# Top-32 attention into a gelu MLP: paired search in two early slots, reordered work in slot 4 and in the first pair of slots

## The chip, the core and the metric

The kernel runs on one core of one Trainium2 chip. The metric is the device time of one execution in microseconds (us), and the time of a kernel is the median over its runs. A separate, profiled execution gives the trace: it records the instructions of each engine with start and duration. The engines are TensorE (PE, whose weight loads are listed as PEld), VectorE (DVE), ScalarE (ACT), GpSimd (POOL) and SyncE (SP, which issues most of the DMAs here).

## The reference

Attention over 8 batches and 8 heads, with 576 positions of 64 numbers, in which each row keeps only its 32 largest scores; the heads are then joined to rows of 512 numbers, and these go through a two-layer MLP with the quick gelu:

```python
scores = scale * q @ k.T                              # (8, 8, 576, 576), scale = 1/sqrt(64)
kth = np.partition(scores, -32)[..., -32]             # 32nd largest of each row
attn = softmax(where(scores >= kth, scores, -1e9))
x = (attn @ v).transpose(0, 2, 1, 3).reshape(8 * 576, 512)
h = x @ w_in                                          # (4608, 2048)
out = (h * (1 / (1 + exp(-1.702 * h)))) @ w_out       # (4608, 512)
```

All is float32.

## The kernel before

**Slots.** The attention is cut into 144 slots. A slot is one tile of 128 rows for one pair of heads; the last 64 rows of four heads make an "ends" slot, so a batch has 18. For slot n the stages are these, each on one engine:

- PE multiplies q by k into two PSUM tiles `s_ps` (`scores`, L295), and ACT copies them scaled to `sc` (`copy_scores`, L307).
- DVE finds the 32 largest of each row. In slots 0 to 10 `topk` does this on all 576 columns: 8 MAX8 (L317) that each find the next eight values, and 6 MATCH_REPLACE8 (L320) that remove them. From slot 11 on `topk_of_pairs` does it on pairs of columns: DVE takes the `greater` of columns j and j + 288 (L336), POOL the `lesser` by two integer operations on the bit patterns (L339 in `pair_up`, L349 in `pair_rest`); then 8 MAX8 and 6 removals on the greater, 4 MAX8 and 2 removals on the lesser (288 columns each, L366 and L369), and two small reductions that merge both lists and give the bound (L373, L378).
- POOL derives the row's bounds `cut` and `low` (`bounds`, L410 and L411, in the early slots; `lows`, L399, for paired slots, whose `cut` comes from DVE).
- ACT masks what lies below the bound (`mask`, L423) and takes the exponentials with their sums (`exps`, L431).
- The sum is inverted on DVE (`invert`, L439 and L441). In the early slots `divide` has POOL make a diagonal matrix of the inverses (L448), with which PE turns the probabilities (`turn_main`, `turn_ends`, L468 and L471) and ACT copies the result `pt` out (L476). In paired slots POOL multiplies the probabilities themselves (`normalize`, L454), ACT splits them into 16-bit halves (`split`, L490), and two DMAs by way of DRAM turn them (`turn_by_dma`, L498).
- PE multiplies by v (`values`, L526; `values_at`, L557), and ACT copies the result into `xT` (L539, L574).

**MLP.** When 128 rows of x are complete for all heads they make a `Block`. `hidden` computes four blocks of 128 hidden features (two for two blocks at a time) into a PSUM tile `ph` (32 matmuls, L618); `tanh` runs on ACT (L640, with a copy of h at L643); `gate` multiplies, either on DVE (L655) or, with `aside`, on POOL (L652, L653); `project` adds the product with w_out to the block's tile `po` (8 matmuls at L673). After 16 feature blocks `po` is complete, ACT copies it out as `ob` (L681) and a DMA stores it.

**PSUM.** `ps_s` has two tiles for scores, `ps_t` has two for turned tiles, values, and some `ph`, `ps_h` has one for `ph`, and `ps_p` one for `po`. A block whose projection begins while `ps_p` holds another takes `ps_h`; while `ps_h` is so taken, `hidden` uses `ps_t`.

**Weights.** Both weight matrices come as 32 pieces that are loaded during slots 0 to 11 and rounded there: `size` (L151), `low` (L154) and `sign` (L153) on ACT, `shift` (L152) on DVE, and two `finish` operations on POOL (L144 and L147). The helper `finish_one` issues the next of the queued finish operations.

**Order.** Each engine works through its instructions in the order in which the program emits them; the kernel writes that order by hand. `slot(n)` emits one early slot: exponentials of n-1, score copies of n+1, then the search of n with pieces of POOL's work between its steps, then PE's turns and values. `two_slots(n)` does the same for slots n and n+1 from n = 11 on; its first call, at n = 11, has `opens` set. SETTLED is 10, PAIRED 11, TURNS 4. `later` holds loads and preparations by slot. `stay_warm` issues matmuls whose result nobody reads. The engines' instructions wait for each other on semaphores where data or a buffer is needed.

Of the kernel before, what the change touches and what calls it, by code (L numbers as in the profile page):

```python
# [11 lines left out]
F32 = mybir.dt.float32  # L12
# [6 lines left out]
P = 128  # L19
# [11 lines left out]
def kernel(  # L31
# [52 lines left out]
    TURNS = 4  # L84
    SETTLED = 10
    PAIRED = SETTLED + 1
    assert D == 64 and 2 * TAIL == P and C == NP * P and C == PIECE and B % 2 == 0
    assert TOPK == 32 and NP == 4 and NF == 4 and NG == 4 and CC == 4

# [241 lines left out]
    def pair_up(n):  # L331

        sc = st[n]["sc"]
        a, b = sc[:, :, 0:HALF], sc[:, :, HALF:S]
        greater[n] = lefts.tile([P, 2, HALF], F32, name="greater", tag="left")
        nc.vector.tensor_tensor(out=greater[n][:], in0=a, in1=b, op=ALU.max)  # L336
        lesser[n] = raws.tile([P, 2, HALF], F32, name="lesser", tag="raw")
        whole = lesser[n][:].bitcast(I32)
        nc.gpsimd.tensor_tensor(out=whole, in0=a.bitcast(I32), in1=greater[n][:].bitcast(I32), op=ALU.subtract)  # L339
        unpaired.append(n)  # L340
# [10 lines left out]
    def topk_of_pairs(n):  # L351

        top = st[n]["top"] = small.tile([P, 2, 2 * TOPK], F32, name="top2", tag="top")
        cut = st[n]["cut"] = small.tile([P, 2], F32, name="cut")
        first, few = greater.pop(n), lesser.pop(n)
        left = lefts.tile([P, 2, HALF], F32, name="left2", tag="left")

        def found(r, i, written=False):
            if r < TOPK // 8:
                at = (8 * r + TOPK) % (TOPK + TOPK // 2)  # L360
                return top[:, i, at : at + 8]
            end = 2 * TOPK - 8 * (r - TOPK // 8) - TOPK
            return top[:, i, end - 1 : end - 9 : -1] if written else top[:, i, end - 8 : end]

        def largest(src, r, i):
            nc.vector.max(found(r, i, True), src[:, i, :])  # L366

        def remove(to, src, r, i):
            nc.vector.match_replace(to[:, i, :], found(r, i), src[:, i, :], LOWEST)  # L369

        def merge():
            both = top[:, :, 0:TOPK].rearrange("p i (s k) -> p i k s", s=2)
            nc.vector.tensor_reduce(  # L373
                out=top[:, :, TOPK + TOPK // 2 :], in_=both, axis=mybir.AxisListType.X, op=ALU.max
            )

        def bound():
            nc.vector.tensor_reduce(  # L378
                out=cut[:], in_=top[:, :, TOPK + TOPK // 2 - 1 :], axis=mybir.AxisListType.X, op=ALU.min, negate=True
            )  # L380

        ops = []
        for r in range(TOPK // 8):
            ops += [lambda r=r, i=i: largest(left if r else first, r, i) for i in range(2)]
            if r < TOPK // 8 - 1:
                ops += [lambda r=r, i=i: remove(left, left if r else first, r, i) for i in range(2)]
        ops += [lambda: pair_up(n + 1) if n + 1 < N else None]
        for r in range(TOPK // 8, TOPK * 3 // 16):
            ops += [lambda r=r, i=i: largest(few, r, i) for i in range(2)]
            if r == TOPK // 8:  # L390
                ops += [lambda r=r, i=i: remove(few, few, r, i) for i in range(2)]
        return ops + [merge, bound]
# [9 lines left out]

    def bounds(n):

        if n >= PAIRED:
            return lows(n)
        top = st[n]["top"]
        cut = st[n]["cut"] = small.tile([P, 2], F32, name="cut")
        low = st[n]["low"] = small.tile([P, 2], F32, name="low")
        nc.gpsimd.tensor_scalar(cut[:], top[:, :, TOPK - 1], -1.0, None, op0=ALU.mult)  # L410
        nc.gpsimd.tensor_tensor(out=low[:], in0=top[:, :, TOPK - 1], in1=top[:, :, 0], op=ALU.subtract)  # L411
# [245 lines left out]
            )  # L657
        to_project.append((th, g, blocks))

    def project(put_off_leaving=False):  # L660

        gT, fs, blocks = to_project.pop(0)
        for x in blocks:
            if not x.done:
                home = "ps_h" if "ps_p" in in_use else "ps_p"
                in_use.append(home)
                x.home = home
                pool_of, tag = (ps_h, "ph") if home == "ps_h" else (ps_p, "po")
                x.po = pool_of.tile([P, C], F32, name="po", tag=tag)
        i = 0  # L670
        for f in fs:
            for x in blocks:
                nc.tensor.matmul(  # L673
                    x.po[:], lhsT=gT[:, i * P : (i + 1) * P], rhs=wout[:, f, :], start=(x.done == 0), stop=(x.done == FC - 1)
                )
                x.done += 1
                i += 1

        def leave(x):
            ob = thp.tile([P, C], F32, name="ob", tag="th")  # L680
            nc.scalar.mul(out=ob[:], in_=x.po[:], mul=0.5 / RAISE**2)  # L681
            for on, to in x.rows:
                nc.sync.dma_start(to, ob[on, :])

        for x in blocks:
            if x.done == FC:
                in_use.remove(x.home)
                leaving.append(lambda x=x: leave(x))
        if not put_off_leaving:
            leave_all()  # L690
# [125 lines left out]
    def slot(n):  # L816

        todo = later.pop(n, [])
        for fn, args in todo:
            if fn is not prepare and fn is not prepare_by_dma:  # L820
                fn(*args)
        preparing = [(fn, args) for fn, args in todo if fn is prepare or fn is prepare_by_dma]
        some = [round_piece(x) for x in by_slot.get(n, [])] if n else early
        if n == 0:
            for piece in some:
                piece["low"]()
                piece["sign"]()
        else:
            bounds(n - 1)
            exponentials(n - 1, bring_all if n % 4 == 1 else lambda: None)  # L830
            copy_scores(n + 1)
            bring_all()
            while signs:
                signs.pop(0)()
            if 1 < n <= TURNS:
                turn_main(n - 2)
                turn_ends(n - 2)
            for piece in some:
                piece["size"]()
            tanh(False)  # L840
        for i, op in enumerate(topk(n)):
            op()
            if i == 2:
                for _ in range(min(3 if n >= TURNS else 6, len(unfinished))):
                    finish_one()
            if i == 5:
                if n > 0:
                    divide(n - 1)
                while unfinished:
                    finish_one()  # L850
            if i == 10:
                gate(False)
        if n == SETTLED:
            pair_up(n + 1)
            pair_rest()
        for piece in some:
            piece["shift"]()
            unfinished.extend(piece["finish"])
        if n < NP:
            for fn, args in preparing:  # L860
                fn(*args)
        if n >= TURNS:
            turn_main(n - 1)
            turn_ends(n - 1)
        if n > 0:
            for piece in some:
                piece["low"]()
        scores(n + 2)
        if n == SETTLED:
            copy_scores(n + 2)  # L870
        if n == 0:
            return
        for i, piece in enumerate(some):
            if n == TURNS and i > 0:
                signs.append(piece["sign"])
            else:
                piece["sign"]()
        idle = not ready and n < TURNS
        if 1 < n <= TURNS:
            values(n - 2, put_off if n == TURNS else None)  # L880
        if n >= TURNS:
            values(n - 1, put_off)
        if n >= NP:
            for fn, args in preparing:
                fn(*args)
        if n > PROJECTS and may_project(2):
            project(n == SETTLED)
        if idle:
            stay_warm(8)
        hidden()  # L890
# [12 lines left out]
    def two_slots(n):  # L903
# [27 lines left out]
        def measure(m):  # L931
            if live(m):
                lows(m)
            pair_rest()
            gate(aside)

        def project_one():
            if may_project(0):
                project(True)

        if opens:
            bounds(n - 1)
            gate(aside)
        if ahead:
            scores(n + 2)
# [26 lines left out]
        for piece in some:  # L972
            piece["shift"]()
            piece["low"]()
            piece["sign"]()
            unfinished.extend(piece["finish"])
        if live(n - 1):
            split(n - 1)
        begin(todo[0])
# [32 lines left out]
            turn_by_dma(n)  # L1012
        tanh(aside)
        measure(n + 1)
        project_one()
        leave_all()

# [38 lines left out]
```

## Time and profile before

| | |
|---|---|
| runs before | 1456.97, 1457.24, 1457.88 us; median 1457.24 |
| profiled execution | 1456.39 us, of which the span of the trace is 1454.6 |
| granted clock of TensorE, mean | 0.986 of full speed |
| first search of slots 1, 2, 3, 4, 5, 6 begins at | 19.72, 30.30, 41.21, 52.13, 63.13, 76.43 us |
| first pair of slots (11 and 12) | about 133 to 165 us |
| a pair of slots later on | about 18.8 us |

Times in a trace are counted from the start of its span. A line of the timeline gives start, duration, engine, line, operation, out<-in and tile, with xcount where several are joined, and in brackets the engine's idle time before it and who ended that. The chain of waits is followed back from the last instruction of its stretch: at each step to what released it, or to the instruction before it on its engine. Engines that share a stretch overlap, so a chain tells which of them set the end, and busy shares alone do not.

### The profile page before, as it was taken

To read this page: it belongs to the slowest core of one execution; us is meant where nothing else is said; L and a number is where in the kernel's file an instruction comes from. 1 tells how busy PE (TensorE), PEld (TensorE's weight loads), DVE (VectorE), ACT (ScalarE), POOL (GpSimd) and SP (SyncE) were. 2 spreads that over 40 slices of the span, in tenths; PEclk is the share of its full clock that TensorE was granted. 3 is DMA by queue.
4 is the path that set the end of the run, shared out by engine and by line. 5 is a ranking of instruction groups with operands and counts; after the bars stand their busy time and mean duration, and the time that the engine had idled before them with its cause. 6 is when DMAs were issued, how large, how long until landed. Compare 5 with 4: busy or idle time off the path is not lost.

```text
span 1454.6 us, 29079 instructions
## 1 busy us (share of the span) xinstructions
PE 1416.5 (97%) x9524; PEld 996.4 (68%) x9524; DVE 1362.5 (94%) x4681; ACT 1158.9 (80%) x1862; POOL 977.6 (67%) x1177
## 2 busy tenths in 40 slices
PE   7789799999999999999999999999999999999998
PEld 5667466777666667777666667777666667777665
DVE  7999999999999999999999999999999999999910
ACT  6998787888888887888888888888878888777730
POOL 3788766766677777666777777766777767667610
PEclk8899899999999999999999999999999999999999
DMA  7442467777777867777677767767677776645430
GB/s 224 136 161 75 127 154 191 189 189 180 176 198 184 188 170 191 186 198 177 170 194 182 183 170 195 202 174 189 166 203 189 180 182 179 161 133 130 138 89 15
DMA packets 521272, 244.40 MB, mean 168 GB/s; under 512 B 457376, under 2 KB 495264, under 8 KB 521120
## 3 DMA queue, kind: packets, MB, share of 16 engines
q1 hardware_dynamic: 520688, 242.25, 64.4%
q8 instruction: 75, 1.23, 0.3%
q14 instruction: 77, 0.63, 0.2%
q10 hardware_dynamic: 432, 0.30, 0.1%
HBM read 45.09 MB, written 103.42 MB: 102 GB/s over the span
## 4 chain that ended last, share of the span: by engine, by line
PE 87%; DVE 10%; ACT 2%; POOL 0%; issue 0%; DMA 0%; DVEq 0%; POOLq 0%; ACTq 0%
PE ph L618 33%; PE po L673 32%; PE o L557 10%; PE s_ps L295 10%; DVE top L317 4%; DVE left L320 3%; DVE top L366 1%; DVE left L369 1%; ACT sc L490 0%; ACT sc L423 0%; ACT pr L431 0%; DVE wout L152 0%; PE none L169 0%; ACT sc L307 0%; DMA pt<-rows 0%
## 5 line engine op out<-in xcount | busy, mean ns | idle before, releaser
L618 PEld LDWEIGHTS ph<-xT,win 128*128 128x128 f32 x3520 | 484.2, 191 | 85.2 <-issue 54.6
L618 PE MATMUL ph<-xT,win 128*128 128x128 f32 (+1 forms) x3520 | 537.1, 309 | 0.5 <-ACT xT L574 0.5
L673 PE MATMUL po<-wout,th 128*128 128x512 f32 x1152 | 521.0, 595 | 5.6 <-POOL wout L147 5.6
L490 ACT COPY sc<-pr 128x2304 uint16<-128x2304 uint16 x134 | 283.1, 2113 | 170.3 <-POOL pr L454 170.3
L673 PEld LDWEIGHTS po<-wout,th 128*128 128x128 f32 x1152 | 213.6, 191 | 219.0 <-issue 205.8
L366 DVE MAX8 top<-left 128x8 f32<-128x288 f32 x798 | 323.2, 446 | 0.0
L339 POOL TENSOR_TENSOR lesser<-sc,greater 128x576 int32<-128x576 int32 x133 | 188.4, 1417 | 179.8 <-DVE greater L336 179.8
L454 POOL TENSOR_SCALAR pr<-pr,rden 128x576 f32<-128x576 f32 x268 | 196.6, 746 | 126.7 <-DVE top L373 77.7
L369 DVE MATCH_REPLACE8 left<-top,left 128x288 f32<-128x288 f32 x532 | 231.3, 442 | 0.0
L431 ACT ACTIVATE pr<-sc,low 128x576 f32<-128x576 f32 x288 | 220.8, 774 | 0.0
L366 DVE MAX8 top<-lesser 128x8 f32<-128x288 f32 x532 | 214.9, 445 | 0.0
L423 ACT ACTIVATE sc<-sc,cut 128x576 f32<-128x576 f32 x288 | 207.4, 774 | 6.2 <-POOL cut L410 6.2
L307 ACT ACTIVATE sc<-s_ps 128x576 f32<-128x576 f32 x288 | 170.9, 648 | 34.2 <-PE s_ps L295 32.6
L349 POOL TENSOR_TENSOR lesser<-lesser,sc 128x576 int32<-128x576 int32 x133 | 187.8, 1412 | 0.1
L295 PE MATMUL s_ps<-qk_t 64*128 64x288 f32 (+1 forms) x1280 | 183.7, 433 | 0.5 <-ACT qk_t L218 0.3
L653 POOL TENSOR_TENSOR th<-th,h 128x512 f32<-128x512 f32 x131 | 167.5, 1279 | 10.9
L295 PEld LDWEIGHTS s_ps<-qk_t 64*128 64x128 f32 (+1 forms) x1280 | 100.2, 179 | 79.2 <-issue 59.0
L557 PE MATMUL o<-pt,v_l 128*64 128x128 f32 (+1 forms) x2400 | 145.8, 265 | 2.1 <-DMA pt<-rows 1.9
L557 PEld LDWEIGHTS o<-pt,v_l 128*64 128x64 f32 x2400 | 121.4, 137 | 29.5 <-issue 17.7
L336 DVE TENSOR_TENSOR greater<-sc 128x576 f32<-128x576 f32 x133 | 131.9, 992 | 0.0
L652 POOL TENSOR_SCALAR th<-th 128x512 f32<-128x512 f32 x131 | 81.5, 622 | 59.7 <-ACT th L640 59.7
L640 ACT ACTIVATE th<-ph 128x512 f32<-128x512 f32 x144 | 85.5, 593 | 38.0 <-PE ph L618 33.9
(78 smaller groups left out, 1365.5 us busy)
## 6 DMA issues: line engine op xcount, KB each, us to landing
rows<-sc SPq DMA_DIRECT2D x134, 576.0 KB, 3.2
qk_rows<-halves SPq DMA_DIRECT2D x48, 256.0 KB, 2.8
qk_l<-in_q_dram SPq DMA_DIRECT2D x64, 128.0 KB, 3.4
raw<-in_moe_w_in_dram SPq DMA_DIRECT2D x16, 512.0 KB, 4.7
v_l<-in_v_dram SPq DMA_DIRECT2D x32, 256.0 KB, 3.7
raw<-in_moe_w_out_dram SPq DMA_DIRECT2D x16, 512.0 KB, 3.5
out_dram<-ob SPq DMA_DIRECT2D x32, 256.0 KB, 2.9
qk_l<-in_k_dram SPq DMA_DIRECT2D x62, 128.0 KB, 3.4
```

The source lines that it names most:

```text
L295: nc.tensor.matmul(ps[i][rows, c, 0:HALF], lhsT=qT[b, hps[p]][on, cols], rhs=kT[b, hps[p]][on, FIRST[i] + c * HALF : FIRST[i] + (c + 1) * ...
L339: nc.gpsimd.tensor_tensor(out=whole, in0=a.bitcast(I32), in1=greater[n][:].bitcast(I32), op=ALU.subtract)
L349: nc.gpsimd.tensor_tensor(out=whole, in0=whole, in1=b.bitcast(I32), op=ALU.add)
L366: nc.vector.max(found(r, i, True), src[:, i, :])
L369: nc.vector.match_replace(to[:, i, :], found(r, i), src[:, i, :], LOWEST)
L423: nc.scalar.activation(sc[:, i, :], sc[:, i, :], AF.Prelu, bias=cut[:, i : i + 1], alpha=HUGE)
L431: nc.scalar.activation(pr[:, i * S : (i + 1) * S], sc[:, i, :], AF.Exp, bias=low[:, i : i + 1], accum_out=den[:, i : i + 1],)
L454: nc.gpsimd.tensor_scalar(pr[:, i, :], pr[:, i, :], st[n]["rden"][:, i : i + 1], 1.0, op0=ALU.mult, op1=ALU.mult)
L490: nc.scalar.copy(out=halves, in_=pr[:].bitcast(U16).rearrange("p (k h) -> p h k", h=2))
L557: nc.tensor.matmul(o[j * D : (j + 1) * D, cols], lhsT=main[:, j, c, :] if c < NF else tail[:, j, :], rhs=pt[:, MAIN[j] + c if c < NF else ...
L618: nc.tensor.matmul(ph[:, i * many * P : (i + 1) * many * P], lhsT=win[:, c, f * P : (f + 1) * P], rhs=xs[:, first : first + step * (many - ...
L673: nc.tensor.matmul(x.po[:], lhsT=gT[:, i * P : (i + 1) * P], rhs=wout[:, f, :], start=(x.done == 0), stop=(x.done == FC - 1))
```

## The change

Three things are done.

Slots 1 and 2 (`EARLY`) search with `topk_of_pairs`. Their greater is taken at the end of slots 0 and 1 and their lesser on POOL right after the bounds of the slot before; the lesser lies in the pool of the scores. `bounds` of slots 0 and 10 move from the next slot to this place too.

In slot 4 two of the three `low` of the weight pieces are emitted ahead of the turns of slot 3, whose copies run on ACT.

In the first pair the third piece among the waiting ones is finished on POOL within `measure(11)`, in place of a gate, and the last piece is finished right after its rounding; the gate is emitted later, with an extra call at slot 14. At the end of that pair `project(True, 1)` projects the second in the queue, which is block 2's first quarter, ahead of block 1's last. Block 2's `po` therefore takes `ps_h`, since `ps_p` still holds block 1's.

```diff
+    EARLY = (1, 2)
+    by_pairs = lambda n: n in EARLY or PAIRED <= n < N
@@ pair_up
-        lesser[n] = raws.tile([P, 2, HALF], F32, name="lesser", tag="raw")
+        home, tag = (scp, "sc") if n in EARLY else (raws, "raw")
+        lesser[n] = home.tile([P, 2, HALF], F32, name="lesser", tag=tag)
@@ topk_of_pairs
-        ops += [lambda: pair_up(n + 1) if n + 1 < N else None]
+        ops += [lambda: pair_up(n + 1) if PAIRED < n + 1 < N else None]
@@ bounds
-        if n >= PAIRED:
+        if by_pairs(n):
@@ project
-    def project(put_off_leaving=False):
-        gT, fs, blocks = to_project.pop(0)
+    def project(put_off_leaving=False, which=0):
+        gT, fs, blocks = to_project.pop(which)
@@ slot
-            bounds(n - 1)
+            if not by_pairs(n):
+                bounds(n - 1)
...
-        for i, op in enumerate(topk(n)):
+        for i, op in enumerate(topk_of_pairs(n) if n in EARLY else topk(n)):
...
-            if i == 5:
+            if i == (10 if n in EARLY else 5):
...
-        if n == SETTLED:
+        if by_pairs(n + 1):
+            bounds(n)
             pair_up(n + 1)
             pair_rest()
...
+        lows_of = [piece["low"] for piece in some] if n > 0 else []
+        if n == TURNS:
+            for _ in range(2):
+                lows_of.pop(0)()
         if n >= TURNS:
             turn_main(n - 1)
             turn_ends(n - 1)
-        if n > 0:
-            for piece in some:
-                piece["low"]()
+        for low in lows_of:
+            low()
@@ two_slots, measure(m)
+            if opens and m == n:
+                finish_one()
+                finish_one()
+                pair_rest()
+                return
             pair_rest()
             gate(aside)
+            if m == SETTLED + 4:
+                gate(aside)
@@ two_slots
         if opens:
-            bounds(n - 1)
             gate(aside)
...
             unfinished.extend(piece["finish"])
+        while unfinished:
+            finish_one()
...
         measure(n + 1)
+        if opens:
+            project(True, 1)
         project_one()
```

## The prediction

> **What bounds the kernel now.** First the page's busy times, then the windows that cut the span by stage (columns after the stretch: its length, busy us and instructions of PE, PEld, DVE, ACT, POOL; granted clock; DMA share; GB/s).
>
> ```profile
> PE 1416.5 (97%) x9524; PEld 996.4 (68%) x9524; DVE 1362.5 (94%) x4681; ACT 1158.9 (80%) x1862; POOL 977.6 (67%) x1177
> ```
>
> ```profile
> 36.00:50.00 14.00, 9.94 (x86) 7.84 (x84) 13.97 (x33) 13.61 (x27) 9.92 (x12) 0.88 0.47 148
> 140.00:155.00 15.00, 9.93 (x67) 6.31 (x65) 14.86 (x47) 11.65 (x20) 14.68 (x15) 0.91 0.16 53
> 155.00:170.00 15.00, 13.62 (x72) 7.55 (x73) 13.43 (x51) 11.09 (x18) 12.81 (x15) 0.75 0.47 135
> 1000.00:1300.00 300.00, 300.00 (x1954) 207.79 (x1953) 296.65 (x1058) 247.31 (x382) 211.24 (x257) 1.00 0.69 176
> ```
>
> The average hides two regimes. In the last row TensorE has no free moment, and from 244.3 us on it waits for nothing. The change edits nothing that PE does after pair 21, so the end moves by as much as PE's arrival at 244.3 does. Before that, DVE (13.97 of 14), ACT (13.61 of 14) and POOL (14.68 of 15) set the pace in turn. Who sets the arrival is read in the chain of waits, cut to 128-250 us (start, duration, piece):
>
> ```profile
> 156.03 1.41 POOL lesser L339
> 157.44 1.45 POOL pr L454 x2
> 158.91 2.11 ACT sc L490
> ...
> 174.86 1.47 POOL pr L454 x2
> 176.36 2.11 ACT sc L490
> 180.15 3.57 PE ph L618 x32
> ...
> 207.29 1.22 PE s_ps L295 x8
> 208.51 1.17 ACT sc L307 x2
> ...
> 220.33 4.53 DMA pt<-rows
> ...
> 243.03 1.24 PE o L557 x20
> 244.29 1.31 PE o L557 x20
> ```
>
> POOL and ACT lead from 156 to 180, PE without a gap from 180 to 208.5 up to the scores of slot 19, and then a score copy, exponentials and a transposing DMA again. The transpose that 244.29 reads was issued at 239.75; at the 4.5 us of its kind it lands at about 244.3. PE and that chain arrive together, so taking work from PE alone brings nothing there: the chain must come earlier too.
>
> **Slots 1 and 2 in pairs.** Out go, per slot, 8 MAX8 on 576 columns at 0.66 and 6 removals at 0.73; with the inversion's 0.26 that is 9.92 us. In come one greater (0.66), 12 MAX8 at 0.36, 8 removals at 0.43 and two reductions (0.22 + 0.19): 9.02 with the inversion. DVE gains 0.9 a slot, 1.8 in all. The new lesser costs POOL 2 x 1.41 a slot, and `lows` 0.5 where the bounds took 0.4; POOL has stood idle 17.6 us before slot 1, and the price shows only as weight pieces finished 2.8 us later, by 39 us, where PE first reads them at 66.41 (the first ph): 0.
>
> ACT does not follow by 1.8. Its idle time ahead of the masks of slots 1, 2 and 3 is 1.73, 0.31 and 0.35. Mask 1 starts 0.9 earlier, but the turned copies that ACT makes at 34.41 need the PE transposes of 32.27, which queue behind `stay_warm` (28.69 to 32.47) and do not move: ACT keeps about 0.5 of it. Then it can close the gaps of 0.31 and 0.35, together 1.2. Against that, the greater of slot 1 runs beside the cut of slot 0: cut took 0.64 beside a DVE shift at 19.24, and 0.21 alone at 137.47, and one caught in a whole greater may come 0.7 later. So X, what reaches slot 4, lies between 0.3 and 1.8 (the latter if ACT follows fully); I take 1.0.
>
> **Low words ahead of the turning copies, slot 4.** Two pieces of 0.61 fill ACT's waits for PE of 0.59 and 1.12 (at 60.19 and 61.89). The first copy slips by 0.6, the second by nothing, and the masks come 1.2 earlier. But the exponentials follow the copy of o, which PE ends at 66.48 in an unbroken run from 58.08, and they start at 66.71 already: what is late next is PE, and the 1.2 is worth 0. Its upper end is 1.2, if PE's run shortens as well.
>
> **First pair on POOL.** POOL is full from 133.9 to 166.4. The change takes the gate (0.61 + 1.27) from before the last weight piece and puts it two measures later, behind the lesser of slot 13 and the normalising of slot 11. That `pr` (157.41) comes up to 1.9 earlier; less what the greater loses to sharing (0.74 when POOL is free, 1.25 to 1.60 beside a POOL instruction), 1.4. The split on ACT (158.91), mask and exponentials follow it, and this wait of DVE goes:
>
> ```profile
> 164.40 0.22 DVE L439 TENSOR_SCALAR some<-den 128x2 f32<-128x2 f32 x1 [1.43 <-ACT pr L431]
> ```
>
> So g = 0.9 to 1.43 at slot 13; I take 1.4. Moving cut and low of slot 10 ahead of the lesser brings mask 10 (137.71) some 2 us forward, on an ACT that then waits 5.20 for `pr`: nothing.
>
> **The projection moved up.** Eight matmuls, 3.44 us, go into this hole of PE:
>
> ```profile
> 153.52 2.07 PE L673 MATMUL po<-wout,th 128*128 128x512 f32 x2 [5.07 <-POOL wout L147]
> ```
>
> They fit (5.07 + 0.53 free), and all later projections run one earlier, until the first half of pair 21, at 235 to 238, has none. That is 3.44 us less for PE before 244.3, where it would then wait for the transpose: 0 by itself. The copies and stores of blocks 2 and 3 come earlier on ACT and SP; 0.59 each on an ACT with 3 us of waits a pair: 0.
>
> A cold clock is saved too: after the hole two po matmuls took 2.07 where two take 1.0, and s_ps 2.29 where it takes 1.24. The Trainium skill ("TensorE: Matmul & The Clock Gate", Part 1) says that an idle window of some 3.4 us halves the clock; filling the hole would give back about 2 us of PE by that rule. PE is not on the chain there, and the sum takes 0.
>
> **The price of moving it.** The projection of block 2 takes the bank `ps_h`, since `ps_p` holds block 1. While it is held, `hidden` of pair 15 goes to `ps_t`, which has two banks. In the issued order the matmuls of that ph then wait for the ACT copy of the turned q. Before, they ran in `ps_h` at 179.99, ahead of the copy:
>
> ```profile
> 179.99 3.74 PE L618 MATMUL ph<-xT,win 128*128 128x128 f32 x32
> 182.19 1.05 ACT L218 COPY qk_t<-tp 128x512 f32<-128x512 f32 x2
> 188.47 1.19 ACT L307 ACTIVATE sc<-s_ps 128x576 f32<-128x576 f32 x2 [1.18 <-PE s_ps L295]
> ```
>
> The first of the two copies ends at 182.7; both ends move together with X + g, so PE loses 182.7 - 180.0 = 2.7 relative to them. Behind it queue the ends' transpose, a projection, and the scores of slots 17 and 19. The copy of scores 17 ended at 189.66 and DVE took its greater at 190.07: of 2.7, 2.3 reach DVE there, and at slot 19 (copy ends 209.66, greater 209.78) another 0.3. Price 2.65; the lower end is 0 (if ACT reaches that copy before PE is ready), the upper 2.7.
>
> **Sum.** Gain at the scores of slot 19, hence at 244.3: 1.0 + 1.4 - 2.65 = -0.2. The profiled run, 1456.39 (span 1454.6 and 1.79 around it), becomes 1456.6; the median of the runs lies 0.85 above the profiled one, so 1457.4. The own range of this case: X 0.3 to 1.8 and g 0.9 to 1.43 give a gain of -1.45 to +0.6, so 1456.6 to 1458.7; with the 1.2 of slot 4 in full, 1455.4.
>
> **Rivals.** R1, faster: the price is not paid, because ACT reaches the q copy in time or DVE has room, and PE comes 3.44 + 1.0 earlier to 244.3, chain and all: 1457.24 - 4.4 = 1452.8. For it: 87% of the chain is PE, PE idles 5.6 us where the projection goes, and there are DVE waits of 1.43 and 0.88 to give. Against it: ACT has mask and exponentials (2.9 us) to do between h and that copy, whatever comes earlier; and the transpose at 244.3 has no slack. Without the price, but with the transpose deciding, it is 1457.24 - 2.4 to - 3.2: 1454.0 to 1454.8.
>
> R2, slower: the bank wait decides and nothing stands against it. The place is pair 15, the price 2.65, and it decides as soon as X + g falls below it. If ACT follows the early search with nothing (X = 0) and the first pair loses to sharing what the gate gave up (g = 0), the end is 1457.24 + 2.65 = 1459.9, and 1460.8 with the 0.9 that one greater loses at 1.60 for 0.74. For it: POOL was full for 32 us in the first pair, and all its work is still there. The Trainium skill ("GPSIMD Engine Reference", table of the engine's data, row on the SBUF interfaces) says that POOL contends with DVE instructions that read two SBUF inputs, which greater does; the rows above agree (1.25 to 1.60 against 0.74). If both new greater were slowed like that, the sum would be 2 x 0.86 higher, 1459.1.
>
> R3, no effect: ACT and PE absorb the early slots (X = 0.3) and g - 2.65 leaves 1.2 to 1.7 too little: within 0.2% again, 1458.2.
>
> **How the numbers follow.** 0.2% of the time is 2.9 us, about what a measurement of this kernel can tell from no change; the bounds are 1454.3 and 1460.2. The case of the sum has 0.41 and R3 0.05, both within. R1 has 0.34: 0.31 beyond the bound, 0.03 at its ends of 1454.3 to 1454.8. R2 has 0.20: 0.17 beyond, 0.03 at 1459.9. So faster 0.31, same 0.52, slower 0.17. The range takes in R1's and R2's times: 1452.8 to 1460.8.
>
> **What would show it.** Slot 3's first MAX8 at 39.4 to 40.9 instead of 41.21 (X). The wait of 1.43 at 164.40 gone and no 5.07 on PE near 150 (g, the projection). A PE wait of about 2.7 ahead of pair 15's ph with ACT's q copy as releaser, and a DVE wait of about 2.3 at the greater of slot 17: without these two, the price is wrong and the time is near 1454. PE's wait near 241 before the transposes, about 3.4, shows that the moved projection is not on the path; if PE has none there and pt comes early, R1 is right.

## The result, and the profile after

The changed kernel takes 1464.12 us (median of 5, 1462.66 to 1464.63); before took 1456.97 in the same runs. The ratio is 1.0046, 95% interval 1.0031 to 1.0061: 7.2 us slower. The forecast was 1457.4, range 1452.8 to 1460.8. The profiled execution of the changed kernel took 1462.66 us, its span 1460.9.

The busy times hardly move, so the time went into waits:

```profile
PE 1418.3 (97%) x9524; PEld 997.6 (68%) x9524; DVE 1362.9 (93%) x4703; ACT 1160.6 (79%) x1862; POOL 987.3 (68%) x1181
```

The windows of the changed kernel, with the stretches shown of before and one more (columns as there):

```profile
36.00:50.00 14.00, 10.51 (x88) 8.43 (x83) 13.90 (x36) 13.92 (x28) 12.54 (x15) 0.88 0.67 200
140.00:155.00 15.00, 13.52 (x70) 8.12 (x64) 14.83 (x52) 11.00 (x18) 14.77 (x15) 1.00 0.12 45
155.00:170.00 15.00, 11.02 (x69) 6.78 (x66) 14.90 (x52) 13.13 (x23) 11.65 (x15) 0.81 0.62 172
230.00:245.00 15.00, 8.66 (x32) 5.01 (x32) 14.83 (x54) 6.99 (x11) 10.21 (x14) 0.77 0.84 187
1000.00:1300.00 300.00, 300.00 (x1959) 207.78 (x1952) 296.74 (x1058) 247.44 (x382) 211.81 (x257) 1.00 0.69 177
```

and that one more stretch of before:

```profile
230.00:245.00 15.00, 14.98 (x101) 10.14 (x101) 14.83 (x54) 11.08 (x18) 11.46 (x16) 1.00 0.76 192
```

The hole at 140-155 is filled as meant (PE 9.93 to 13.52 us, clock 0.91 to 1.00). But at 230-245, where PE had no free moment, it now works 8.66 of 15, at a clock of 0.77. The chain of waits of the changed kernel, cut to 125-250, leads to it:

```profile
171.94 1.48 POOL pr L457 x2
173.44 2.11 ACT sc L493
...
179.90 3.84 PE ph L621 x32
...
207.31 1.22 PE s_ps L297 x8
208.53 1.18 ACT sc L309 x2
...
231.55 1.48 POOL pr L457 x2
233.05 2.11 ACT sc L493
236.46 1.28 POOL th L656
237.78 6.18 PE po L676 x8
```

From the hidden part at 179.90 up to 207.3 PE does what it did in the chain of before, at the same time (207.29 there, in an execution whose first search began 0.71 later). Then a new end appears, a gate on POOL and behind it a projection. In the timeline (start, duration, engine, line, operation, tile; in brackets the idle time before it and who ended that), PE of the changed kernel:

```profile
227.60 3.84 PE L621 MATMUL ph<-xT,win 128*128 128x128 f32 x32
237.78 6.18 PE L676 MATMUL po<-wout,th 128*128 128x512 f32 x8 [6.34 <-POOL th L656]
```

its ACT and POOL:

```profile
235.07 0.59 ACT L643 ACTIVATE th<-ph 128x512 f32<-128x512 f32 x1
235.75 0.62 POOL L655 TENSOR_SCALAR th<-th 128x512 f32<-128x512 f32 x1 [0.89 <-ACT th L643]
236.46 1.27 POOL L656 TENSOR_TENSOR th<-th,h 128x512 f32<-128x512 f32 x1
```

and of before two lines of PE in the same place, then the two gates of POOL that lie around them and follow each other:

```profile
227.58 3.84 PE L618 MATMUL ph<-xT,win 128*128 128x128 f32 x32
231.25 3.60 PE L673 MATMUL po<-wout,th 128*128 128x512 f32 x8
207.32 1.27 POOL L653 TENSOR_TENSOR th<-th,h 128x512 f32<-128x512 f32 x1
236.43 1.28 POOL L653 TENSOR_TENSOR th<-th,h 128x512 f32<-128x512 f32 x1
```

This is the end of pair 19. Before, two quarters lay in the queue of projections there: the last one of block 3, whose gate had run at 207.32, and the first one of block 4, whose gate is issued just ahead of this projection and ran at 236.43. PE projected the old one at once. In the changed kernel every projection since the first pair has run one earlier, so the old quarter is gone and the only one left is that whose hidden part PE itself has just ended (231.4). Its tanh waits on ACT behind the split of slot 20 (233.05), its gate follows on POOL, and PE stands idle for 6.34 us. The eight matmuls then take 6.18 instead of 3.60, at a granted clock of 0.60 (237.8 to 244.0; the clock comes to 0.50 in such stretches, and matmuls at it are called cold here).

### The profile page after: what moved, and what is told of

It is laid out like the page before. It is cut to its first block, busy times and chain, and to the rows that moved or that the text cites. A ratio compares the mean times of both kernels' runs of the same rounds, so it can differ in the third digit from the quotient of the medians.

```text
span 1460.9 us, 29106 instructions
## 1 busy us (share of the span) xinstructions
PE 1418.3 (97%) x9524; PEld 997.6 (68%) x9524; DVE 1362.9 (93%) x4703; ACT 1160.6 (79%) x1862; POOL 987.3 (68%) x1181
## 4 chain that ended last, share of the span: by engine, by line
PE 86%; DVE 11%; ACT 2%; issue 1%; POOL 0%; DVEq 0%; POOLq 0%
PE ph L621 33%; PE po L676 32%; PE s_ps L297 10%; PE o L560 10%; DVE top L319 3%; DVE left L322 2%; DVE top L369 2%; DVE left L372 1%; DVE lesser L372 1%; DVE greater L338 1%; ACT sc L493 0%; ACT sc L309 0%; DVE wout L154 0%; DVE win L154 0%; POOL pr L457 0%
## 5 line engine op out<-in xcount | busy, mean ns | idle before, releaser
L369 DVE MAX8 top<-left 128x8 f32<-128x288 f32 x810 | 328.2, 447 | 0.0
L372 DVE MATCH_REPLACE8 left<-top,left 128x288 f32<-128x288 f32 x540 | 234.9, 443 | 0.0
L369 DVE MAX8 top<-lesser 128x8 f32<-128x288 f32 x540 | 218.1, 445 | 0.0
L352 POOL TENSOR_TENSOR lesser<-lesser,sc 128x576 int32<-128x576 int32 x135 | 190.9, 1414 | 0.2
L656 POOL TENSOR_TENSOR th<-th,h 128x512 f32<-128x512 f32 x131 | 167.7, 1280 | 11.2 <-POOL th L655 0.4
```

Of the source, the lines that this page charges most:

```text
L352: nc.gpsimd.tensor_tensor(out=whole, in0=whole, in1=b.bitcast(I32), op=ALU.add)
```

## The experiments

Three theories. **D**: the queue of projections runs dry at the end of pair 19, and that is most of the loss. **B**: the bank wait at pair 15, which the prediction priced at 2.65, is the loss and grows on its way. **P**: the early paired search or POOL's new order costs later what it gains.

The start of the first search differs from one execution to the next (8.70 to 10.15 us), so the traces are compared from there. The table gives the time from the start of the first search to the greater of slot 11 (DVE), to the scores of slots 19, 23 and 25 (PE) and to the end of the span, and the median of the runs.

| kernel | greater 11 | scores 19 | scores 23 | scores 25 | end | median us | ratio to before (95%) |
|---|---|---|---|---|---|---|---|
| before | 123.58 | 197.81 | 232.38 | 251.51 | 1445.19 | 1456.97 | |
| changed | 122.84 | 198.54 | 238.76 | 258.48 | 1452.20 | 1464.12 | 1.0046 (1.0031-1.0061) |
| a: no moved projection | 123.06 | 195.84 | 230.41 | 250.29 | 1443.97 | 1454.83 | 0.9991 (0.9983-1.0000) |
| b: one held back | 123.08 | 198.79 | 232.96 | 253.44 | 1447.13 | 1459.11 | 1.0019 (1.0010-1.0028) |
| c: projection alone | 123.76 | 202.59 | 243.05 | 262.77 | 1456.42 | 1467.91 | 1.0078 (1.0065-1.0090) |
| d: early slots alone | 122.90 | 197.17 | 231.75 | 252.50 | 1446.29 | 1456.59 | 1.0001 (0.9993-1.0010) |
| e: first pair alone | 123.23 | 196.60 | 231.16 | 250.32 | 1443.95 | 1455.20 | 0.9988 (0.9980-0.9997) |
| f: low words alone | 123.73 | 197.95 | 232.51 | 251.57 | 1445.64 | 1456.78 | 1.0000 (0.9991-1.0009) |
| i: dry queue alone | 122.17 | 196.33 | 235.99 | 255.70 | 1449.40 | 1461.61 | 1.0032 (1.0019-1.0045) |
| j: bank wait alone | 124.17 | 202.89 | 237.05 | 256.93 | 1450.70 | 1461.54 | 1.0031 (1.0019-1.0042) |
| g: before again | 124.21 | 198.37 | 232.95 | 252.18 | 1445.85 | one run, 1457.59 | |
| h: early slots again | 123.03 | 197.23 | 231.79 | 251.94 | 1445.58 | one run, 1456.53 | |

Before had a median of 1456.67 beside a to d and of 1456.77 beside e, f, i and j. From the scores of slot 25 to the end all twelve take 1193.6 to 1194.1 us, so what a kernel has lost by then it has lost for good. A common start does not remove all scatter: before, c, g, i and j have the same program up to slot 11, and their greater of slot 11 lies at 122.17 to 124.21. Shorter stretches repeat to about 0.1, and the last part goes by those.

**a, the changed kernel without the moved projection.**

```diff
         measure(n + 1)
-        if opens:
-            project(True, 1)
         project_one()
```

> The changed kernel without the projection of block 2 at the end of the first pair; all else as changed. Theory D (the queue of projections runs dry: the projection at the end of pair 19 is of the quarter just gated, so TensorE waits 6.34 us for POOL and then works at a cold clock): that wait goes, and with it the bank wait at pair 15, so that the gains of the early slots and of the first pair stay: 2.2 to 2.9 us under before, 1454.0 to 1454.8. Theory B (the bank wait at pair 15 is the loss, and it grows on its way): the same time, since the bank wait goes too. Theory P (the early slots or POOL's new order cost later what they gain): not under before, 1457 or more.

Measured: 1.84 us under before, 9.3 under the changed kernel, and no wait of PE for a gate near 236. The moved projection brings the whole loss. P falls: the other parts together gain, if less than the 2.2 expected.

**b, the changed kernel with one projection held back.**

```diff
-        project_one()
+        if n != SETTLED + 9:
+            project_one()
```

> The changed kernel, and at the end of pair 19 no projection is issued, so that the next one comes in pair 21 between its two hidden parts, as before. The moved projection and the bank wait at pair 15 stay. Theory D: the 6.34 us wait and the cold matmuls after it go, and the time is that of before within 0.7 us: 1456.3 to 1457.7, with a wait of up to 2.9 us left at the held projection. Theory B: the loss stays, 1462 or more.

Measured: 5.0 us under the changed kernel, but 2.4 over before, 1.4 more than D allowed for. PE in its trace:

```profile
238.41 3.70 PE L676 MATMUL po<-wout,th 128*128 128x512 f32 x8 [2.77 <-POOL th L656]
245.89 1.09 PE L560 MATMUL o<-pt,v_l 128*64 128x128 f32 x16 [1.37 <-DMA pt<-rows]
```

The quarter still comes 2.77 us after PE is ready, but PE has done the next hidden part in between, and that is the saving. B alone falls, since the bank wait is still there. But b lies 4.3 over a, and b differs from a by the moved projection with its bank wait and by the 2.77 that is left: both causes are at work, which i and j then part.

**c, before with the moved projection alone.** `project` has its argument `which` as in the change; besides that:

```diff
         measure(n + 1)
+        if opens:
+            project(True, 1)
         project_one()
```

> Before, with only the projection of block 2 added at the end of the first pair. Theory D: nothing makes up for the bank wait, so the scores of slot 19 come 2.65 to 2.9 us later than before, and the dry queue at pair 19 adds its 6.3: about 9 us over before, 1465.5 to 1466.5. Theory B: 2.65 to 2.9 us over before, 1459.6 to 1459.9, without a long wait at pair 19.

Measured: 11.2 us over before. The dry queue shows the same wait of 6.34, with 6.42 for the eight matmuls. The scores of slot 19 come 4.8 later rather than 2.65 to 2.9, which j explains.

**i, the dry queue alone.**

```diff
         project_one()
+        if n == SETTLED + 7:
+            project_one()
```

> Before, with one projection more at the end of pair 17, so that the queue of projections holds only the quarter just gated at the end of pair 19, as in the changed kernel; block 2 stays in ps_p, there is no projection in the first pair's hole and no bank wait at pair 15. Theory D: TensorE waits about 6 us for POOL's gate near 232 to 238 and is cold after it; the scores of slot 23 come 5.6 us later and the end 5.5 to 6.5 us later, about 1462.5. Theory B: no loss from it, within 1 us of before; all of the loss is the bank wait's.

Measured: 4.84 us over before, without block 2 in `ps_h` and without a moved projection. Its PE:

```profile
235.65 5.64 PE L673 MATMUL po<-wout,th 128*128 128x512 f32 x8 [5.37 <-POOL th L653]
```

This is 0.7 short of the lower end that D gave, with a wait that is 1.0 shorter. From the scores of slot 19 to those of 25 it loses 5.67 (59.37 for 53.70); the changed kernel loses 6.24 there (59.94). So on the stretch of the wait i does what D said; its trace was 1.48 ahead of before at the scores of slot 19, up to which the two programs do not differ.

**j, the bank wait alone.** c with the hold of b, shown against before and without `which`:

```diff
+        if opens:
+            project(True, 1)
-        project_one()
+        if n != SETTLED + 9:
+            project_one()
```

> Before, with the projection of block 2 moved into the first pair, and the projection at the end of pair 19 held back, so that the queue does not run dry: the bank wait at pair 15 by itself, with nothing gained ahead of it. In the run with the projection alone the scores of slot 19 came 4.8 us later than before (counted from the first search): 2.66 of wait and some 1.7 of matmuls at a cold clock after it. Theory D: the end comes 4.5 to 5.5 us later, 1461 to 1462. The price of the prediction, 2.65 alone: 1459.5. Theory B: all of the 11.2 us that the projection alone cost: 1467.

Measured: 4.77 us over before, as D had it. Its PE at pair 15:

```profile
183.83 5.47 PE L618 MATMUL ph<-xT,win 128*128 128x128 f32 x32 [2.65 <-ACT qk_t L218]
```

PE waits 2.65, where the prediction read off 2.7. What was left out is the clock behind it: 5.47 for 32 matmuls that took 3.74, at a granted clock of 0.58 from 184 to 188. The scores of slot 19 come 4.56 later by it, counted from the greater of slot 15 (40.40 for 35.84); from there to those of slot 25 only 0.34 is added, so the held projection costs little. Dry queue (4.84) and bank wait (4.77) add up to 9.6 of the 11.2 of c.

**d, the early slots alone.** Before with `EARLY`, `by_pairs` and the lines of `pair_up`, `topk_of_pairs`, `bounds` and `slot` that go with them; slot 10 as before:

```diff
+        if n + 1 in EARLY:
+            bounds(n)
-        if n == SETTLED:
+        if by_pairs(n + 1):
             pair_up(n + 1)
             pair_rest()
```

> Before, with only the paired search in slots 1 and 2. The first search of slot 6 came 1.45 us earlier in the changed kernel than before, but the first search of all began 0.71 us earlier too, which no edit explains. Theory D counts 0.75 for the early slots: 1456.2, range 1455.5 to 1456.6. If the 1.45 are all of the change: 1455.5. Theory P: no gain, 1457 or more.

Measured: no difference (1.0001). At the scores of slot 19 it is 0.64 ahead of before, and then PE waits for the transposing DMA of slot 20:

```profile
244.69 1.09 PE L560 MATMUL o<-pt,v_l 128*64 128x128 f32 x16 [1.64 <-DMA pt<-rows]
```

**e, the first pair's new order on POOL alone.** The changed kernel without its other parts:

```diff
-    EARLY = (1, 2)
+    EARLY = ()
...
-        if n == TURNS:
-            for _ in range(2):
-                lows_of.pop(0)()
...
-        if opens:
-            project(True, 1)
```

> Before, with only the first pair's new order on POOL (the bounds of slot 10 ahead of the lesser, the last weight pieces ahead of the gate, the gate two measures later), no moved projection, no early paired search, low words as before. Theory D counts 1.47 us gained at the greater of slot 15 and no bank wait, so the scores of slot 19 come 1.3 to 1.5 us earlier, counted from the first search of the kernel; at the transposing DMA near 244 up to 1 us of it may be lost: 0.4 to 1.5 under before. Theory P (POOL's new order costs later what it gains): no change or slower.

Measured: 1.57 us under before, and PE has no wait for that DMA. Of this change it is the part that pays.

**f, the low words alone.**

```diff
+        lows_of = [piece["low"] for piece in some] if n > 0 else []
+        if n == TURNS:
+            for _ in range(2):
+                lows_of.pop(0)()
         if n >= TURNS:
             turn_main(n - 1)
```

> Before, with only two low words of slot 4 ahead of the turning copies. All theories: no change, within 0.5 us, since the exponentials of slot 4 start when TensorE has ended o.

Measured: 0.01 us. As expected.

**g and h, second traces of before and of d.**

> Before, unchanged, for a second trace. If the start of the first search (9.41 us in the first trace; 8.70 to 10.15 in those of the other kernels) and the wait for the transposing DMA of slot 20 near 244 (none in the first trace) are matters of the single execution, they differ here by several tenths; if they belong to the kernel, they are 9.41 and none again.

> Before with only the paired search in slots 1 and 2, for a second trace. In the first one TensorE waited 1.64 us for the transposing DMA of slot 20, which took back the 0.64 that the early slots had brought to the scores of slot 19. If that wait belongs to this kernel, it is within 0.3 of 1.64 again; if to the execution, it is not. The greater of slot 11, counted from the first search, is at 122.8 to 123.1 again if the early slots' gain is real, and at 123.4 or more if it was the execution's.

Measured: the first search begins at 9.95 and 9.12, so that start is a matter of the execution. Before again has no wait for the DMA near 244; h has one of 1.04, after 1.64 in d. The greater of slot 11 lies at 122.84 to 123.08 in all five traces with early pairs and at 122.17 to 124.21 in the seven without (mean 123.55). That is a difference of 0.6, under a scatter of 2 us among the seven. Nearer to the edit it is clear: counted from the first search, the search of slot 3 begins at 30.75 to 30.77 in the five and at 31.80 to 31.81 in the seven, that of slot 4 at 42.01 to 42.03 and at 42.72. So the early slots bring 1.04 to slot 3 and 0.70 to slot 4, in every trace; the scatter comes in behind them.

## Why the prediction was wrong

**Right up to the scores of slot 19.** The sum there was 1.0 + 1.4 - 2.65 = -0.2. Measured, changed against before: X 0.74 at the greater of slot 11 (0.70 at slot 4; 1.0 was taken), g 1.47 (from there to the greater of slot 15: 36.92 instead of 38.39), price 2.94 (from there to the scores of slot 19: 38.78 instead of 35.84): -0.73. The last two repeat: 36.92 to 36.93 in changed, a and b, and 38.32 to 38.43 in the eight traces without the new order of the first pair; 38.78 in changed and b, and 35.84 or 35.85 in the eight traces without the moved projection. By itself (e) the new order gave 0.86 on its stretch (37.53), so part of g comes only together with the early slots. In the working of X, the operations listed for a paired slot add up to 9.09, not 9.02, which is 0.83 a slot and not 0.9.

Most signs announced are there too. The first MAX8 of slot 3 is at 39.45, in the span forecast, of which 0.71 is the earlier first search. The DVE wait of 1.43 is gone, and of PE's 5.07 in the hole 1.48 is left. These two lines of the timeline of the changed kernel, of PE and of DVE, are the price. PE's own wait is shorter than the 2.7 announced because PE comes to it later: its matmuls at 165.7 to 170.3 are cold (granted clock 0.50), where before they were not.

```profile
179.90 3.84 PE L621 MATMUL ph<-xT,win 128*128 128x128 f32 x32 [1.08 <-ACT qk_t L220]
189.78 0.76 DVE L338 TENSOR_TENSOR greater<-sc 128x576 f32<-128x576 f32 x1 [2.55 <-ACT sc L309]
```

**Wrong at the step after it.** The prediction said of the projections that run one earlier until pair 21: "That is 3.44 us less for PE before 244.3, where it would then wait for the transpose: 0 by itself." It took a missing instruction for a saving that at worst is worth nothing, and did not ask what the projections ahead of it now wait for. A queue that is served one earlier each time is one shorter, and before it held exactly one quarter more than was just being gated. The term put at 0 is -6.34 (wait) - 2.58 (6.18 for 3.60) + 3.44 (the projection that is gone) = -5.5; measured between the scores of 19 and 23, 40.22 instead of 34.57, it is 5.65, and 6.24 up to slot 25. Undone (b) it gives back 5.0, and by itself (i) it costs 4.84. The prediction had read that PE and the chain arrive at 244.3 together, and used it in one direction only: work taken from PE alone brings nothing. A wait added to PE goes to the end, and that was not asked. Half of its sign for R1 came true all the same: PE of the changed kernel has no wait before the products with v at 248.6 and 249.8, but because PE itself came late, and not because the transposing DMA came early (issued at 239.75 in both).

**A term of the right kind but too small: the bank wait.** The rival R2 named it as what could decide, at 2.65. It is 2.94 in the changed kernel, and 4.56 by itself (j; 4.77 at the end), because 32 cold matmuls follow it there, 1.73 longer. In the changed kernel the cold matmuls lie ahead of it, at 165.7 to 170.3, and shorten the wait. The prediction knew the cold clock from the hole at 148-153, but used it only where the change removes an idle stretch, not where it makes one; the hole is filled and warm now, and PE is cold from 165.7 instead.

**Right: the parts put at nothing.** The low words (f) are worth 0.01. That POOL and DVE's greater slow each other, which the prediction weighed against the change, cost less than feared: the two new greater took 0.74 and 0.87, not 1.60. What was stretched there was POOL, whose cut beside the first took 1.31 instead of 0.64, the 0.7 that the prediction allowed for. The prediction's "0.74 when POOL is free" is not quite what before shows either: the greater at 160.65 took 0.74 with a gate of POOL beside it, and the gate's first operation took 1.18 instead of 0.61.

**Left open.** The 0.7 of the early slots does not reach the end in d, and in a it is not clear of the scatter (a 1454.83, e without the early slots 1455.20). In the four traces a, b, d and h, with early pairs, the transposing DMA of slot 20 landed 5.3 to 6.2 us after its issue and PE waited 0.77 to 1.64 for it; in before, its second trace, e and f, without them, PE did not wait, and in j, also without, 0.78. What slows that transfer was not found. Of c's 1.6 us beyond the sum of i and j, 0.5 lies between the scores of 19 and 25 (6.48, for 5.67 and 0.34), where c waits 6.34 and i 5.37 for the gate. In c, i and the changed kernel the waiting projection starts 30.5 us after the scores of slot 19; PE of i comes to it 0.96 later than the others, having one projection more behind it, and so waits less. The rest lies in stretches ahead of slot 19, where i's trace was ahead without a cause in its program.

**The better versions.** e beats before (0.9988, interval 0.9980 to 0.9997) and the changed kernel; a has the lowest median, with an interval that ends at before's time.

## What to carry to other kernels

Moving a step of a queue forward moves every later step of that queue forward too: find the place where the backlog ends, and ask there whether the next item is ready when its turn comes. An instruction that disappears from a busy stretch is no gain if the one that stood behind it has a later input; list who releases each step in its new place, not only at the place of the edit. And price a new wait of TensorE with the slower matmuls that may follow it: 1.7 to 2.8 us here, though none after one wait of 2.77.

## What the hardware showed that was not expected

How long TensorE may wait before its clock falls is not one number here. After a wait of 2.77 us eight matmuls took 3.70 at a granted clock of 1.00 (b; j has the same), while waits of 5.37 and 6.34 were followed by 5.64 and 6.18 for the same eight, with a clock of 0.50 at their start. Two waits of 0.97 and 2.65 with 0.66 us of transposes between them were enough too (5.47 for 3.74, j). So were two waits with 1.9 us of work between them in the changed kernel, and there the clock was still 1.00 after the first:

```profile
162.71 0.33 PE L224 MATMUL tp<-ident,qk_l 128*128 128x128 f32 x1 [2.68 <-ACT qk_t L220]
165.74 1.98 PE L560 MATMUL o<-pt,v_l 128*64 128x128 f32 x16 [1.14 <-DMA pt<-rows]
```

And one wait can end both ways: near 102 to 105 us the same 16 transposes follow 2.59 to 2.64 us of waiting in e, i, j and g, and the clock of the 1.5 us behind it was 0.98, 0.82, 0.60 and 0.60. The Trainium skill ("TensorE: Matmul & The Clock Gate", Part 1) puts the idle window at some 3.4 us. For a single long wait the runs fit that roughly: 2.77 left the clock up, and 3.25 in the hole of the first pair of e, behind one of 0.57, did not (2.08 for two matmuls, at 0.50). But j and the changed kernel show that some work between two shorter waits need not keep the clock up.

The start of the first search, which no edit touches, varied from 8.70 to 10.15 us over twelve traces. That is nearly as much as the largest gain of any part here (1.57, e), so small effects were read on short stretches between two points inside the trace.
